# Sign of the float64 weights carried through the fp32 conversion by a parametric ReLU, with a new order of issue

## The chip, the cores and the metric

The kernel runs on one core of one Trainium2 chip. The core has TensorE (PE, with its weight loads as PEld), VectorE (DVE), ScalarE (ACT), GpSimd (POOL) and SyncE (SP), which issues the transfers. The metric is the time of one execution in microseconds on the device. The kernel before took 516.62 us, the median of 3 runs (513.7 to 518.07).

## The reference

Three blocks follow one another. An attention over 16 heads (2 batches of 8) of 768 positions and 64 dimensions masks by hash buckets; its output is laid out as two sequences of 768 x 512. A gated convolution and a mix of neighbours with a squared ReLU follow.

```python
q_bits = (einsum('bhsd,dk->bhsk', q, proj) > 0); k_bits = ...
mask = q_bucket[..., :, None] == k_bucket[..., None, :]
scores = where(mask, scale * q @ k.T, -1e9); scores -= max(scores, -1)
attn = exp(scores) / (sum(exp(scores), -1) + 1e-09);  a = attn @ v
gate = sigmoid(sum_k conv_w[k] * shifted(x, k));  y = (gate * (x @ w_val)) @ w_out
xk = mu_k * y + (1 - mu_k) * y_prev;  xr = mu_r * y + (1 - mu_r) * y_prev
v = max(xk @ w_k, 0) ** 2 @ w_v;  out = sigmoid(xr @ w_r) * v
```

The weights `w_val`, `conv_w`, `w_out`, `w_k`, `w_v` and `w_r` come as float64, and no engine computes in that type. The kernel reads each as pairs of 32-bit words, the low word (`raw[:, :, 0]`) and the high word (`raw[:, :, 1]`), and makes fp32 of them.

## The kernel before, in words

**Attention, about the first 270 us.** The heads run one after another. For each head and each of 6 tiles of 128 keys, `smax` (L685, L687) makes scores without the low parts on PE, whose maximum over all keys DVE takes out of PSUM; the 6 maxima become a shift in `mxr` (L692) that PE turns into a row (`shift`, L699, L703). Later `scores` (L713, L714) makes the exact scores of half a tile of queries, ACT takes the exponential into one of 6 buffers of a ring (L715), POOL adds up the denominators (L717, L719) and `values` (L725) multiplies by v on PE. `sums`, `spread` and `norm` (L745, L757 to L761, L775, L778) divide. Beside this, pairs of later heads are loaded, transposed (L550, L552), split into a high and a low part (`prep_hi` L556 on ACT, `prep_lo` L559 on DVE), hashed to bits (`prep_bits`: PE L564, DVE L567, ACT L569) and copied into place by transfers (`fill`, `penalties`).

**The conversion of the weights** runs in the same time: 28 tiles of 128 x 512 (`weight(i, part)`) and one of 20 x 128 for `conv_w` (`vectors`). Part 0 loads a tile into one of two `raw` buffers. Part 1, `cvt_high` (L387), is an ACT copy of the high word, read as fp32, times 2^-112, which moves the exponent by the difference of the two biases and leaves it three places too far right. Part 2, `cvt_low` (L390), is an ACT copy that scales the low word's leading bits down to an integer. Part 3, `cvt_join`, is on DVE in three steps: shift left by 3 and clear the sign bit (L394), add the low word's bits (L396, shown as CUSTOM_DVE_ANT_0), and take the sign bit from the high word and OR it in (L397).

**After it,** `split_weight` (L416, L417) splits each fp32 weight into two fp32r parts: ACT copies the high part, then DVE (tiles 0 to 7, 18, 19) or POOL (the others) subtracts. The front of the first half sequence (taps of the convolution L447, `front_val`, gate L450 to L452, `mid_out`, mixes L461 to L468) is woven into heads 13 to 15 and what follows them. From about 318 us on, four half sequences run as long chains of matmuls (`acc3`, L427, three per product of split operands).

**The order.** Every engine works through its own queue in order. `_order` gives each event a slot from constants (`K_...`) plus corrections by name in two tables (`MOVED`, and `SWING` for what repeats by head), sorts by slot, and the events are issued in that order.

Of the kernel before, what the change touches and what calls it, by code (L numbers as in the profile page):

```python
# [51 lines left out]
K_END = (3.3, 10.5, 7.4)  # L52
K_OPEN = -0.2
K_SPLIT = (5.2, 1.8)
K_SPLIT2 = (1.6, 1.75)
K_CLOSE = 8.6

K_XS = (6.3, 0)
K_TAP = (9, 0.6)
K_VAL = (2.7, 1)  # L60
K_SIG = (13.7, 0.1)
K_GATE = (14, 0.6)
K_OUT = (17.6, 0.7)
K_MIX = (8.5, 9, 0.5, 1, 13, 1.2, 0.7)
NC, NTAP, NSPLIT, NRAW, NSPLIT2 = 4, 5, 8, 12, 28
K_SPLITR = (10.2, 5.9)
# [267 lines left out]
def fused_kernel(ctx: ExitStack, tc: tile.TileContext, q, k, v, proj, w_val, conv_w, w_out,  # L334
                 mu_k, mu_r, w_k, w_v, w_r, cols, sel, out):
    nc = tc.nc
# [49 lines left out]
    def cvt_high(raw, dst):  # L386
        nc.scalar.activation(out=dst, in_=f32(raw[:, :, 1]), func=AF.Copy, scale=2.0 ** -112)  # L387
# [623 lines left out]
```

## Time and profile before

| | |
|---|---|
| median of 3 runs | 516.62 us (513.7 to 518.07) |
| the profiled execution's own time | 515.39 us |
| its span, first to last instruction | 513.6 us |
| PE, DVE, ACT, POOL busy in the span | 94%, 71%, 61%, 39% |
| TensorE clock granted, mean of the span | 0.995 of full speed |

Busy shares are means over stages with different limits; the stretches matter more. PE's matmuls overlap one another and their ends are modelled, so a busy PE can still be slowed. A wait is put down to the engine that released it last.

### The profile page before, as it was taken

Reading aid. Unit: us, or ns where it says so; the run is one execution under the profiler, and the core shown is the slowest. Engines: PE = TensorE matmul, PEld = TensorE weight load, DVE = VectorE, ACT = ScalarE, POOL = GpSimd, SP = SyncE. Lnnn points to the kernel's source line nnn. Section 1 sums busy time; section 2 is a strip of 40 time slices with the busy share of each in tenths; the row PEclk is TensorE's granted clock in tenths of the full one; section 3 lists DMA queues with packets and bytes.
Section 4 is the critical chain, followed back from the end, with each engine's and each line's share of the span. In section 5 each row is a group of like instructions: output and inputs, shape, how many; then the busy total and the mean of one; then the engine's idle time right before and its main releaser. Section 6 shows DMA issues by size and latency. Waiting matters only on the chain.

```text
span 513.6 us, 7300 instructions
## 1 busy us (share of the span) xinstructions
PE 482.3 (94%) x2545; PEld 360.6 (70%) x2545; DVE 363.7 (71%) x551; ACT 312.8 (61%) x632; POOL 198.7 (39%) x205
## 2 busy tenths in 40 slices
PE   8799989899999989999896998999999999999997
PEld 5655565564656556455575986899889998899885
DVE  4858889798999969989999992269522992138113
ACT  5868678686778687778756586275522852236221
POOL 6476656673857757667772136400000000000000
PEclk9999999999999999999999998999999999999999
DMA  7498968879789783780000000001000010001001
GB/s 171 112 213 228 231 166 187 186 202 209 198 194 217 192 208 121 201 205 2 0 2 1 2 1 2 0 1 61 1 0 2 1 63 0 1 0 63 0 1 61
DMA packets 43522, 47.57 MB, mean 93 GB/s; under 512 B 29250, under 2 KB 33886, under 8 KB 43486
## 3 DMA queue, kind: packets, MB, share of 16 engines
q1 hardware_dynamic: 43486, 47.12, 36.8%
q8 instruction: 20, 0.33, 0.3%
q14 instruction: 16, 0.13, 0.1%
HBM read 24.35 MB, written 3.15 MB: 54 GB/s over the span
## 4 chain that ended last, share of the span: by engine, by line
PE 48%; DVE 9%; ACT 3%; issue 2%; DMA 1%; POOL 1%; SPq 0%; DVEq 0%; ACTq 0%; POOLq 0%
PE bank L427 24%; PE smb L427 16%; PE bank L725 3%; DVE gp L447 3%; PE bank L713 2%; PE smb L685 1%; PE bank L714 1%; ACT ring L715 1%; DMA raw<-in_moe_w_v_dram 1%; DVE xT L778 1%; DVE mx L687 1%; DVE w L417 1%; POOL w L417 1%; DVE tm L462 1%; DVE big L439 1%
## 5 line engine op out<-in xcount | busy, mean ns | idle before, releaser
L719 POOL TENSOR_TENSOR acc<-acc,ring 128x384 f32<-128x384 f32 x128 | 131.1, 1041 | 38.1 <-ACT ring L715 35.3
L715 ACT ACTIVATE ring<-bank 128x384 f32<-128x384 f32 x192 | 89.9, 494 | 33.4 <-PE bank L714 32.4
L687 DVE TENSOR_REDUCE mx<-smb 128x1 f32<-128x768 f32 x96 | 88.6, 951 | 17.6 <-PE smb L685 16.8
L713 PE MATMUL bank<-big,big 128*128 128x384 f32 x192 | 75.0, 391 | 6.9 <-ACT ring L715 6.3
L725 PE MATMUL bank<-ring,vn 128*64 128x385 f32 x384 | 77.8, 504 | 0.9 <-ACT ring L715 0.9
L427 PE MATMUL bank<-big,w 128*128 128x384 f32 x224 | 75.5, 337 | 0.7 <-POOL w L417 0.7
L935 DVE TENSOR_TENSOR gp<-gp,bank 128x384 f32<-128x384 f32 x32 | 17.5, 550 | 75.7 <-ACT gp L934 75.7
L713 PEld LDWEIGHTS bank<-big,big 128*128 128x128 f32 x192 | 36.0, 188 | 42.8 <-ACT ring L715 22.7
L714 PE MATMUL bank<-big,big 97*128 97x384 f32 x192 | 65.0, 339 | 0.0
L427 PE MATMUL smb<-wv,kk 128*128 128x512 f32 x176 | 60.5, 391 | 0.0
L685 PE MATMUL smb<-big,big 88*128 88x384 f32 x192 | 51.0, 354 | 6.2 <-DVE mx L687 4.6
L934 ACT ACTIVATE gp<-bank 128x384 f32<-128x384 f32 x32 | 15.7, 491 | 60.7 <-PE bank L427 60.6
L717 POOL TENSOR_TENSOR acc<-ring 128x384 f32<-128x384 f32 x32 | 30.3, 950 | 47.3 <-ACT ring L715 47.2
L725 PEld LDWEIGHTS bank<-ring,vn 128*64 128x64 f32 x384 | 22.4, 135 | 31.2 <-issue 25.7
L685 PEld LDWEIGHTS smb<-big,big 88*128 88x128 f32 x192 | 32.8, 189 | 15.6 <-DVE mx L687 8.9
L427 PEld LDWEIGHTS bank<-big,w 128*128 128x128 f32 x224 | 42.0, 188 | 1.4 <-POOL w L417 1.4
L447 DVE SCALAR_TENSOR_TENSOR gp<-xT,vec,gp 128x384 f32<-128x384 f32 x64 | 41.0, 672 | 0.3
L427 PEld LDWEIGHTS smb<-wv,kk 128*128 128x128 f32 x176 | 33.2, 188 | 6.8 <-DVE kk L938 0.2
L714 PEld LDWEIGHTS bank<-big,big 97*128 97x128 f32 x192 | 36.5, 190 | 0.0
L427 PE MATMUL smb<-w,kk 128*128 128x512 f32 x88 | 34.5, 392 | 0.0
L427 PE MATMUL bank<-big,raw 128*128 128x384 f32 x128 | 33.1, 338 | 0.5 <-DVE big L468 0.5
L938 DVE TENSOR_TENSOR kk<-gp,kk 128x384 fp32r<-128x384 f32 x32 | 18.3, 576 | 20.7 <-ACT kk L937 20.5
(141 smaller groups left out, 896.6 us busy)
## 6 DMA issues: line engine op xcount, KB each, us to landing
big<-hlq SPq DMA_DIRECT2D x14, 384.0 KB
big<-hlk SPq DMA_DIRECT2D x14, 384.0 KB
raw<-in_moe_w_k_dram SPq DMA_DIRECT2D x8, 512.0 KB
raw<-in_moe_w_v_dram SPq DMA_DIRECT2D x8, 512.0 KB
vn<-in_v_dram SPq DMA_DIRECT2D x8, 384.0 KB
qn<-in_q_dram SPq DMA_DIRECT2D x14, 192.0 KB
kn<-in_k_dram SPq DMA_DIRECT2D x7, 384.0 KB
big<-bits SPq DMA_DIRECT2D x28, 96.0 KB
```

Of the source, the lines that this page charges most:

```text
L427: nc.tensor.matmul(out=ps, lhsT=w[a], rhs=xx[c], start=first and j == 0 and m == 0, stop=last and j == n - 1 and m == 2)
L447: nc.vector.scalar_tensor_tensor(out=gp, in0=src, scalar=w, in1=gp, op0=ALU.mult, op1=ALU.add)
L685: nc.tensor.matmul(out=sm[:, hf, 0:HF], lhsT=qd[0:KA, 0, 128 * t:128 * t + 128], rhs=kd[0:KA, 0, HF * hf:HF * hf + HF], start=True, stop=True)
L687: nc.vector.tensor_reduce(out=mxs[n][:, t:t + 1], in_=sm[:, :, 0:HF], op=ALU.max, axis=AX.XY)
L713: nc.tensor.matmul(out=st, lhsT=kd[:, 1, kt], rhs=qd[:, 1, cs], start=True, stop=False)
L714: nc.tensor.matmul(out=st, lhsT=kd[0:KS + 1, 0, kt], rhs=qd[0:KS + 1, 0, cs], start=False, stop=True)
L715: nc.scalar.activation(out=p[:, 0:HF], in_=st, func=AF.Exp, scale=scale)
L717: nc.gpsimd.tensor_add(acc, probs[n, 0, hf][:, 0:HF], p[:, 0:HF])
L719: nc.gpsimd.tensor_add(acc, acc, p[:, 0:HF])
L725: nc.tensor.matmul(out=pvp[n][64 * hf:64 * hf + 64], lhsT=nat["v", n // 2][:, n % 2, t, :], rhs=probs[n, t, hf], start=t == 0, stop=t == N ...
L935: nc.vector.tensor_mul(rl, rl, ps)
L938: (nc.vector if f in V_LO else nc.gpsimd).tensor_sub(kk[:, 1], rl, f32(kk[:, 0]))
```

## The change

`cvt_high` becomes a parametric ReLU with the same factor 2^-112 and a slope alpha of -(2^32) for negative inputs. A negative weight comes out positive and 2^32 times as large, so bit 28 of its pattern is set; the shift left by 3 moves that bit to the place of the sign and drops what stood above. `cvt_join` then needs neither the AND nor the third step: two DVE instructions per tile where there were three. All numbers that give the order are new, by mostly small amounts; the tables change in nearly every row. Lines of the changed file lie 23 further down from the tables on (L394 and L396 are its L420 and L421).

```diff
-K_SPLIT2 = (1.6, 1.75)
-K_CLOSE = 8.6
+K_SPLIT2 = (0.9, 2.05)
+K_CLOSE = 10
...
-K_TAP = (9, 0.6)
+K_TAP = (8.3, 0.6)
...
-    ('prep_bits', 2): -2.5, ('smax', 3, 3): -1, ('prep_hi', 'q', 2): 6, ('prep_t', 2, 'q', 0): -9,
+    ('prep_bits', 2): -2.5, ('smax', 3, 3): -1, ('prep_hi', 'q', 2): 6, ('prep_t', 2, 'q', 0): -11.4,
...
     def cvt_high(raw, dst):
-        nc.scalar.activation(out=dst, in_=f32(raw[:, :, 1]), func=AF.Copy, scale=2.0 ** -112)
+        nc.scalar.activation(out=dst, in_=f32(raw[:, :, 1]), func=AF.Prelu, scale=2.0 ** -112, alpha=-(2.0 ** 32))
...
     def cvt_join(raw, dst):
         t = dst.bitcast(I32)
-        nc.vector.tensor_scalar(out=t, in0=t, scalar1=3, scalar2=0x7FFFFFFF,
-                                op0=ALU.logical_shift_left, op1=ALU.bitwise_and)
+        nc.vector.tensor_single_scalar(out=t, in_=t, scalar=3, op=ALU.logical_shift_left)
         nc.vector.tensor_tensor(out=t, in0=t, in1=raw[:, :, 0], op=ALU.add)
-        nc.vector.scalar_tensor_tensor(out=t, in0=raw[:, :, 1], scalar=-(1 << 31), in1=t,
-                                       op0=ALU.bitwise_and, op1=ALU.bitwise_or)
```

First place, DVE's queue in the steady attention, at the first `spread` of a pair of heads; `w` is a weight tile, `rec` and `rhl` are the reciprocals of `spread`, `xT` the normed output. Before:

```order
L394 TENSOR_SCALAR w<-w 128x512
L396 ISA w<-raw,w 128x1024
L397 SCALAR_TENSOR_TENSOR w<-raw,w 128x512
L757 RECIPROCAL rec<-dn 128x12
L760 CAST rhl<-rec 128x12
L761 TENSOR_TENSOR rhl<-rec,rhl 128x12
L559 TENSOR_TENSOR hlq<-t_687,hlq 128x768
L687 TENSOR_REDUCE mx<-smb_116 128x1
L778 SCALAR_TENSOR_TENSOR xT<-pvs,vm,bank_113 64x384 x2
```

The same place in the changed kernel:

```order
L420 TENSOR_SCALAR w<-w 128x512
L421 ISA w<-raw,w 128x1024
L780 RECIPROCAL rec<-dn 128x12
L783 CAST rhl<-rec 128x12
L784 TENSOR_TENSOR rhl<-rec,rhl 128x12
L710 TENSOR_REDUCE mx<-smb_116 128x1
L582 TENSOR_TENSOR hlq<-t_678,hlq 128x768
L801 SCALAR_TENSOR_TENSOR xT<-pvs,vm,bank_113 64x384 x2
```

The third step is gone and a maximum went ahead of a `prep_lo`; the neighbours are otherwise the same. This holds for all 28 tiles.

Second place, DVE's queue at the end of attention, around the last weight tile: `wout` are splits, `big` splits of the input, `gp` taps. Before:

```order
L439 TENSOR_TENSOR big_2292<-xT,big_2292 128x384 x2
L417 TENSOR_TENSOR w<-w,wout_0_2111 128x512
L417 TENSOR_TENSOR w<-w,wout_0_2112 128x512
L439 TENSOR_TENSOR big_2292<-xT,big_2292 128x384
L394 TENSOR_SCALAR w<-w 128x512
L396 ISA w<-raw,w 128x1024
L397 SCALAR_TENSOR_TENSOR w<-raw,w 128x512
L447 SCALAR_TENSOR_TENSOR gp<-xT,vec,gp 128x384
L757 RECIPROCAL rec<-dn 128x12
L760 CAST rhl<-rec 128x12
L761 TENSOR_TENSOR rhl<-rec,rhl 128x12
L447 SCALAR_TENSOR_TENSOR gp<-xT,vec,gp 128x384 x7
```

And in the changed kernel:

```order
L462 TENSOR_TENSOR big_2260<-xT,big_2260 128x384
L780 RECIPROCAL rec<-dn 128x12
L783 CAST rhl<-rec 128x12
L784 TENSOR_TENSOR rhl<-rec,rhl 128x12
L440 TENSOR_TENSOR w<-w,wout_0_2085 128x512
L462 TENSOR_TENSOR big_2260<-xT,big_2260 128x384
L470 SCALAR_TENSOR_TENSOR gp<-xT,vec,gp 128x384
L440 TENSOR_TENSOR w<-w,wout_0_2086 128x512
L420 TENSOR_SCALAR w<-w 128x512
L421 ISA w<-raw,w 128x1024
L470 SCALAR_TENSOR_TENSOR gp<-xT,vec,gp 128x384 x9
```

The reciprocals of heads 12 and 13 now stand ahead of the last two splits and the first tap ahead of the last tile; the taps follow in one run.

Third place, ACT's queue just before the long chains of matmuls, where the splits of `w_k` (`wk`) and `w_r` (`wr`) are made between the mixes (`tm`, `big`) and the ReLUs (`gp`). Before:

```order
L416 CAST wk_1_2652<-w 128x512
L461 ACTIVATE tm<-xT,omm 128x384
L934 ACTIVATE gp<-bank_112 128x384
L465 CAST big_2696<-tm 128x384
L461 ACTIVATE tm<-xT,omm 128x384
L465 CAST big_2696<-tm 128x384
L416 CAST wk_1_2653<-w 128x512
L416 CAST wr_0_2654<-w 128x512
L416 CAST wr_0_2655<-w 128x512
```

And in the changed kernel:

```order
L439 CAST wk_1_2643<-w 128x512
L484 ACTIVATE tm<-xT,omm 128x384
L957 ACTIVATE gp<-bank_112 128x384
L488 CAST big_2667<-tm 128x384
L439 CAST wk_1_2644<-w 128x512
L439 CAST wr_0_2645<-w 128x512
L484 ACTIVATE tm<-xT,omm 128x384
L957 ACTIVATE gp<-bank_114 128x384
L488 CAST big_2667<-tm 128x384
L439 CAST wr_0_2646<-w 128x512
```

The fourth cast of `wk` and the first of `wr` went one step of the mix ahead; POOL subtracts behind each of these casts.

## Rows read from the trace of the kernel before

**Rows 1.** The page: span, busy time by engine, chain that ended last.
```profile
span 513.6 us, 7300 instructions
PE 482.3 (94%) x2545; PEld 360.6 (70%) x2545; DVE 363.7 (71%) x551; ACT 312.8 (61%) x632; POOL 198.7 (39%) x205
PE 48%; DVE 9%; ACT 3%; issue 2%; DMA 1%; POOL 1%; SPq 0%; DVEq 0%; ACTq 0%; POOLq 0%
```

**Rows 2.** Windows: length, busy us of PE, PEld, DVE, ACT, POOL (instructions), clock, DMA.
```profile
0.00:40.00 40.00, 33.54 (x190) 22.12 (x190) 25.59 (x35) 27.00 (x50) 23.51 (x37) 1.00 0.72 169
40.00:140.00 100.00, 92.16 (x511) 54.91 (x513) 86.92 (x114) 75.35 (x154) 64.33 (x64) 1.00 0.82 199
140.00:240.00 100.00, 95.55 (x538) 56.76 (x534) 89.28 (x120) 77.51 (x156) 66.58 (x69) 1.00 0.71 175
240.00:300.00 60.00, 53.18 (x279) 40.04 (x277) 58.88 (x95) 38.79 (x85) 25.65 (x23) 1.00 0.01 1
300.00:318.00 18.00, 16.00 (x73) 13.50 (x73) 9.77 (x17) 14.45 (x30) 10.13 (x8) 0.91 0.00 0
318.00:513.60 195.60, 191.84 (x964) 173.30 (x962) 93.27 (x174) 79.71 (x162) 8.54 (x7) 1.00 0.05 17
```

**Rows 3.** Waits from 20 to 240 us: waiter, releaser, us in total, times, longest.
```profile
PE smb L685 <- DVE mx L687: 3.5, 6, 1.5
PE smb L699 <- DVE mxr L692: 1.6, 2, 1.1
PE bank L745 <- DVE bits L567: 0.5, 2, 0.3
ACT bits L569 <- DVE bits L567: 9.9, 7, 2.7
PE bank L713 <- ACT ring L715: 5.7, 15, 0.9
PE smb L685 <- DMA big<-bits: 1.5, 1, 1.5
```

**Rows 4.** Groups by line and form: count, busy us, mean ns, idle before.
```profile
L713 PE MATMUL bank<-big,big 128*128 128x384 f32 x192 | 75.0, 391 | 6.9 <-ACT ring L715 6.3
L714 PE MATMUL bank<-big,big 97*128 97x384 f32 x192 | 65.0, 339 | 0.0
L397 DVE SCALAR_TENSOR_TENSOR w<-raw,w 128x512 int32<-128x512 int32 x28 | 25.8, 922 | 1.0
L394 DVE TENSOR_SCALAR w<-w 128x512 int32<-128x512 int32 x28 | 16.3, 582 | 2.8 <-ACT w L387 2.7
L387 ACT ACTIVATE w<-raw 128x512 f32<-128x512 f32 x28 | 21.9, 783 | 4.9 <-DMA raw<-in_moe_w_val_dram 2.9 <-DMA raw<-in_moe_w_v_dram 0.7 <-DMA raw<-in_moe_w_k_dram 0.6
L848 ACT ACT_TABLE_LOAD x1 | 1.3, 1283 | 0.0
```

**Rows 5.** Windows of L397 alone on DVE: length, busy us (instructions), clock, DMA.
```profile
40.00:140.00 100.00, 12.66 (x13) 1.00 0.82 199
140.00:240.00 100.00, 11.21 (x13) 1.00 0.71 175
240.00:300.00 60.00, 0.69 (x1) 1.00 0.01 1
```

**Rows 6.** L397's durations (ns min/median/max), and timelines of DVE and POOL (start, us).
```profile
L397 DVE SCALAR_TENSOR_TENSOR w<-raw,w x28: 691/693/1520, 32.1 to 255.5; 128x512 int32<-128x512 int32 x28
172.06 1.52 DVE L397 SCALAR_TENSOR_TENSOR w<-raw,w 128x512 int32<-128x512 int32 x1
172.03 1.01 POOL L719 TENSOR_TENSOR acc<-acc,ring 128x384 f32<-128x384 f32 x1 [1.17 <-ACT ring L715]
...
238.21 0.69 DVE L397 SCALAR_TENSOR_TENSOR w<-raw,w 128x512 int32<-128x512 int32 x1
```

**Rows 7.** Waits from 303 to 319 us, and the window of the slower clock.
```profile
PE bank L427 <- POOL w L417: 2.0, 4, 0.9
314.00:318.00 4.00, 3.85 (x10) 3.04 (x11) 1.38 (x2) 2.33 (x6) 2.26 (x3) 0.57 0.01 2
```

More of the change, by code (lines that the diff above doesn't have):

```diff
@@ new lines @@
+    ('shift', 0, 0): -1.8, ('scores', 1, 5, 0): -1.7, ('scores', 1, 3, 0): -0.6, ('shift', 0, 1): 1.3,
+    ('norm', 0): 0.3, ('scores', 1, 0, 1): -0.3, ('values', 0, 5): 1, ('scores', 0, 5, 1): -0.2,
+    ('weight', 2, 2): 0.5, ('weight', 1, 2): 1, ('weight', 0, 3): 0.5, ('weight', 2, 1): 0.5, ('smax', 1, 4): -0.3,
+    ('scores', 1, 1, 0): -0.8, ('scores', 0, 3, 0): 1, ('values', 0, 2): 0.5, ('scores', 0, 1, 1): 0.7,
+    ('weight', 0, 2): 0.5, ('scores', 0, 2, 0): 0.5, ('weight', 1, 0): 0.1,
@@ new lines @@
+    ('prep_t', 2, 'k', 0): -2.1, ('first_hi', 0, 1): 7, ('values', 15, 3): 7.2, ('smax', 2, 0): -1.2,
+    ('values', 13, 2): 0.2, ('smax', 2, 1): 1.1, ('weight', 0, 1): -17.9, ('values', 15, 0): 5.7,
+    ('spread', 14, 1): 1.3, ('prep_lo', 'k', 2): 3.3, ('fill', 3, 0): 15, ('first_bits', 0): -12.3,
+    ('prep_lo', 'q', 1): 4, ('shift', 1): -1.5, ('warm', 4): -4, ('values', 14, 4): -1.9, ('values', 13, 5): 3.5,
+    ('first_hi', 0, 0): -13.8, ('weight', 3, 0): 5, ('weight', 0, 2): -7.6, ('norm', 11): 0.8, ('weight', 1, 3): 4.4,
@@ new lines @@
+    ('load_qk', 5): -0.3, ('shift', 2): -0.3, ('load_v', 7): 3, ('values', 15, 2): 6.7, ('values', 15, 4): 5.7,
+    ('values', 15, 5): 5.7, ('warm', 8): 0.8, ('weight', 9, 2): -2.4, ('weight', 9, 0): -0.7, ('weight', 9, 1): -1.2,
+    ('weight', 9, 3): -0.7, ('prep_hi', 'q', 5): -0.7, ('shift', 4): -0.3, ('weight', 1, 1): -0.9,
+    ('prep_t', 1, 'k', 0): 0.5, ('weight', 26, 0): -1, ('weight', 17, 2): -1.5, ('smax', 2, 5): 3,
+    ('penalties', 2): 0.3, ('prep_lo', 'q', 6): -0.5, ('weight', 14, 0): -0.1, ('weight', 21, 3): -0.3,
@@ new lines @@
+    ('weight', 8, 0): -1.8, ('weight', 8, 2): -4, ('weight', 8, 3): -0.7, ('prep_hi', 'q', 7): 0.5,
+    ('penalties', 6): 2.6, ('smax', 8, 0): -1.8, ('prep_t', 5, 'k', 0): 0.5, ('smax', 14, 3): 2.7,
+    ('fill', 15, 1): -0.3, ('weight', 24, 3): -1.5, ('weight', 24, 0): -0.7, ('weight', 24, 1): -4.7,
+    ('weight', 24, 2): -2.2, ('load_v', 5): -6.9, ('shift', 0, 0): 1, ('scores', 13, 4, 1): -1.7,
+    ('scores', 14, 0, 0): -0.8, ('scores', 1, 4, 1): -1.3, ('weight', 6, 0): -1, ('scores', 0, 5, 0): -0.6,
@@ new lines @@
+    ('norm', 1): 0.3, ('scores', 11, 5, 1): -1, ('mid_hi', 1, 2): 0.8, ('weight', 18, 0): -1.5,
+    ('scores', 5, 4, 1): 1.3, ('sums', 13): 0.9, ('mid_lo', 1, 1): 1.5, ('front_gate', 2): 1.2,
+    ('weight', 27, 2): 0.3, ('weight', 13, 3): -0.3, ('scores', 4, 3, 0): 1.3, ('fill', 8, 1): 3,
+    ('scores', 8, 4, 1): 1.2, ('vectors', 2): -2, ('scores', 4, 5, 0): 0.5, ('shift', 6): 1,
+    ('prep_t', 3, 'q', 1): 0.3, ('weight', 6, 3): 0.3, ('weight', 18, 2): -0.7, ('mid_hi', 1, 3): 0.7,
+    ('shift', 11): -0.7, ('weight', 21, 2): -0.7, ('scores', 4, 4, 0): 0.8, ('prep_lo', 'k', 6): 0.4,
```

297 lines of the change are left out of this document (148 added, 149 removed).

## The prediction

> **What bounds the kernel now.** I began with the page's busy times and its chain [rows 1]: PE is busy 94% of the span and holds 48% of it on the chain that ended last, DVE 9%. That alone would say that work taken from DVE is worth nothing. So I cut the span into stretches [rows 2]. From 318 us on PE is busy 191.84 of 195.6 us and DVE 93; nothing in this change touches that part. Before it three stretches differ. From 40 to 240 us PE is busy 187.71 of 200 us, DVE 176.20 and ACT 152.86: no engine is full, three in-order queues hand work to each other, and PE is idle for 12.3 us. From 240 to 300 us DVE is busy 58.88 of 60 us and PE only 53.18: here DVE sets the pace. From 300 to 318 us neither does; ACT is busy 14.45 of 18 us and PE waits for POOL [rows 7].
>
> The waits say who holds PE up in the second stretch and its run-up [rows 3]. From 20 to 240 us PE waits for DVE's maxima, shifts and bits for 3.5 + 1.6 + 0.5 = 5.6 us, for ACT's exponentials 5.7 us. Behind ACT stands DVE once more: in each of 7 pairs of heads ACT's scaling of the bits waits for DVE, 9.9 us in all, and ACT's exponentials queue behind it. A wait also costs more than its idle time: the first matmul of a score takes 391 ns and the second, which never waits, 339 ns [rows 4], 192 times 52 ns, or 10.0 us. What a better fed PE could win before 240 us is thus bounded by 12.3 + 10.0 = 22.3 us.
>
> **The change part by part.** *The third step.* 28 instructions of 922 ns, 25.8 us of DVE, go [rows 4]; 23.87 us of that lie from 40 to 240 us and 0.69 us after 240 [rows 5]. DVE's load from 40 to 240 us falls from 176.2 to 152.3 us, that is from 88% to 76%, ACT's level. What is it worth at the end? Between 0 (PE keeps its pace, since it is held by ACT and by its own stream) and 22.3 us (all that PE loses there). I take a value near the named waits. PE's 5.6 us of waits for DVE come in pieces of at most 1.5 us, about as long as one third step that stands ahead in the queue; with a conversion ahead of about two waits in three I let 3.5 us go. ACT's wait for the bits is 9.9 / 7 = 1.4 us each time; one third step less ahead of it saves about 0.7 us, 5 us of ACT's time, and since ACT is busy three quarters of the time I let a third of it reach PE: 1.5 us. Together -5.0 us.
>
> Part of the 922 ns is no work. L397 takes 691 ns at the least and 1520 at the most, and the long one at 172.06 us ran while POOL added from 172.03 us on [rows 6]. So 28 times 0.69, or 19.3 us, is work, and 6.5 us is time held up beside POOL, which the next DVE instruction may meet instead. This is why I stay at 5.0 us and don't go higher. The Trainium skill says of this, in "SBUF — State Buffer", section "SBUF: two separate sides", that a DVE instruction with two SBUF inputs and a GpSimd instruction that reads SBUF lock each other out for a whole instruction; the trace agrees with the 691 and 1520 ns above. By that rule the lock outlives the change, as the add (L396) still takes it, and the saving would be 19.3 / 25.8 of what was counted, 3.7 us instead of 5.0.
>
> *The first step with one operation instead of two.* L394 takes 582 ns on average [rows 4]. The trace holds no shift alone; the nearest row is L394 itself, so I put 0 and bound it by 28 times its whole 0.58 us to either side: -16.3 us of DVE's time if it cost nothing, +16.3 if it doubled. Neither extreme has a reason, since input and output are the same; over the path the ratio taken above (5.0 of 25.8) makes this -3 to +3 us.
>
> *ReLU for copy on ACT.* 28 instructions of 783 ns [rows 4], same shape, factor and operands. I put 0. The bounds are again from the nearest row: -21.9 to +21.9 us of ACT (free or doubled); ACT is a quarter idle, so at most some 7 us of that would reach the end. A table switch would be dearer; it is the fourth rival.
>
> *The stretch led by DVE.* The last tile's third step (0.69 us) goes from it, and that of the tile ahead of it, 0.69 us at 238.21 us [rows 6], hands DVE over to this stretch that much earlier; the only third step behind 240 us is the last tile's [rows 5]. DVE is full here, so both count whole: -1.4 us. The reciprocals that now go first only reorder DVE's work; their gain is that PE's norm of heads 12 and 13 is ready sooner, which I put at 0. What comes late next is the run of taps, which is as long as before.
>
> *The new order before 318 us.* The casts of the fourth `wk` and the first `wr` go one step of the mix ahead on ACT, and so do POOL's subtractions behind them. PE waited 2.0 us in four pieces for these [rows 7]; I take half of it, -1.0 us. The bounds are -2.0 us and, if the ReLUs that now queue behind the casts came late, +1.6 us (two casts, each at most the 0.78 us of L387, the nearest row [rows 4]). Right behind the last of these waits the granted clock was 0.57 on average from 314 to 318 us, partly the lower level of 1.2 GHz, after PE had waited again and again. I don't count on its going.
>
> *All other moves* shift events by at most a few halves of a score tile. Loads and fills stay in the same places between the heads, SP's queue moves with them. I put 0, and -2 to +2 us for what a start with other neighbours may do in the first 40 us, where PE is idle 6.46 us [rows 2].
>
> Sum: -5.0 - 1.4 - 1.0 = -7.4 us against the profiled execution, 515.4 us: 508.0 us. The median of the runs shown is 1.2 us above that execution, which gives 509.2; I say 509 us.
>
> **The rivals.** *1. The time was hidden.* DVE's idle time grows and PE keeps its pace, as ACT's exponentials and PE's stream set it. For it speaks that PE is already busy 95.55 of 100 us from 140 to 240 us and waits for ACT as long as for DVE [rows 2, 3]; against it that ACT itself waits 9.9 us for DVE. Only the 1.4 us at the end remain: 515.4 - 1.4 + 1.2 = 515 us.
>
> *2. DVE set the pace all along.* Of the 23.87 us two thirds come back, 16 us, below the bound of 22.3. For it speak 88% of load on a queue with waits at both ends; against it the named waits, which are a third of that. 515.4 - 16 + 1.2 gives 501 us.
>
> *3. Slower: the transfers come late.* The 16 DMA engines are busy 82% from 40 to 140 us [rows 2], and once there a maximum waited 1.5 us for the bits of the next pair to land [rows 3]. If the heads run on faster while fills and penalties are issued as late as before, PE comes 7.4 / 7 = 1.1 us earlier to each of 7 pairs, and a pair that waits then costs 1.5 + 1.1 = 2.6 us. From three such pairs on (7.8 us) the gain is eaten; with five it is 13.0 - 7.4 = 5.6 us slower, 522 us. Against it: one such wait in seven pairs.
>
> *4. The ReLU isn't in the exponential's table.* Each of 28 conversions would then load a table twice, at 1283 ns [rows 4]: 72 us of ACT. ACT is idle for 47 us from 40 to 240 us [rows 2], so 25 to 72 us would show: 541 to 589 us, in the middle 565. The queue of the changed kernel has still two table loads, at its start and ahead of the first sigmoid, as before, which nearly excludes it. The Trainium skill, "ScalarE: Activation LUTs", section "Table sets: the hidden batching unit", says that functions are loaded in named sets and a change of set costs a load; two loads in both queues agree with one common set.
>
> **How the numbers follow.** The forecast has 0.55, and its own range is 504 to 512 us. Rival 1 has 0.25, rival 2 has 0.11, rival 3 has 0.08, rival 4 has 0.01. From 501 to 517 us takes in the forecast, rival 1 and half of rival 2, and the bounds of the small terms; rival 3 and the far half of rival 2 stay out. About 1%, or 5 us, is what a measurement of this kernel can tell from no change. Faster by more than that: four fifths of the forecast and rival 2 and a little of rival 1, 0.58. Slower: most of rival 3 and rival 4, 0.07. Within 1%: 0.35.
>
> **What would show it.** In the profile after, DVE should have 28 large instructions fewer and some 25 us less busy time, near 338 us; the shift should keep its 582 ns and the ReLU its 783 ns. PE's waits for DVE's maxima from 20 to 240 us should fall from 5.6 to about 2 us, ACT's wait for the bits from 9.9 to about 5, and the last score should come 5 us earlier. Waits of PE for ACT that grow by as much as those for DVE fall would prove rival 1; waits for the bits' transfers in most pairs rival 3; a last score 15 us earlier rival 2. A longer ReLU or shift would make a term of the sum wrong.

## The result, and the profile after

The changed kernel takes 510.46 us (median of 4 runs, 509.83 to 511.14), the kernel before beside it 515.64 us (4 runs): ratio 0.9897, 95% interval 0.9849 to 0.9945, or -5.2 us (509.0 were forecast). Its profiled execution took 510.76 us with a span of 509.0 us; before it was 515.39 and 513.6. Run again later on another chip, the same kernel took 508.69 us, ratio 0.9907 (0.9873 to 0.9942), or -3.0 to -6.5 us; the two medians there differ by 6.6 us (515.31 before). A few runs below took over 1.5% longer than the fastest of the same kernel: the ratios leave them out, the medians don't.

The page after, in the same lines as [rows 1]:

```profile
span 509.0 us, 7262 instructions
PE 485.2 (95%) x2545; PEld 360.1 (71%) x2545; DVE 335.5 (66%) x522; ACT 314.4 (62%) x632; POOL 192.7 (38%) x205
PE 55%; DVE 6%; ACT 5%; DMA 1%; issue 1%; POOL 1%; SPq 0%; ACTq 0%; POOLq 0%; DVEq 0%
```

DVE has 29 instructions and 28.2 us less and holds 6% of the chain, not 9. PE's busy time went up by 2.9 us although it has the same 2545 matmuls; the windows, cut as in [rows 2], tell why:

```profile
0.00:40.00 40.00, 34.19 (x188) 22.11 (x189) 23.19 (x32) 28.37 (x52) 22.28 (x37) 0.96 0.79 186
40.00:140.00 100.00, 94.41 (x516) 55.13 (x516) 74.22 (x102) 75.20 (x152) 61.69 (x66) 0.98 0.82 194
140.00:240.00 100.00, 97.27 (x544) 58.11 (x540) 80.50 (x111) 80.07 (x161) 66.39 (x69) 1.00 0.70 174
240.00:300.00 60.00, 56.14 (x290) 41.86 (x290) 56.00 (x93) 39.88 (x86) 26.11 (x24) 1.00 0.01 1
300.00:318.00 18.00, 15.97 (x76) 13.18 (x76) 9.58 (x17) 13.57 (x28) 11.58 (x10) 1.00 0.01 2
318.00:509.00 191.00, 187.25 (x944) 169.68 (x942) 92.01 (x171) 77.28 (x157) 4.68 (x4) 1.00 0.05 17
```

The clock was 1.00 in both of the first windows of [rows 2] and 0.91 from 300 to 318 us. Now it is 0.96 and 0.98 at the start and 1.00 from 300 to 318: the stretches at the lower level of 1.2 GHz, half of the full 2.4 GHz, have moved into the attention. There a matmul counts as busy for longer (the second one of a score 0.52 us at 124.78 us, 0.34 us at 120.41), so part of PE's higher share is no gain. From 40 to 240 us DVE is busy 154.72 of 200 us, 77%; before it was 88%.

The waits from 20 to 240 us, in answer to [rows 3], and the groups, in answer to [rows 4]:

```profile
PE bank L736 <- ACT ring L738: 5.5, 13, 1.2
ACT bits L592 <- DVE bits L590: 3.5, 6, 1.3
PE smb L708 <- DMA raw<-in_moe_w_k_dram: 1.4, 1, 1.4
PE smb L722 <- DVE mxr L715: 0.7, 2, 0.4
PE smb L708 <- DMA big<-bits: 0.5, 1, 0.5
PE smb L708 <- DVE mx L710: 0.2, 1, 0.2
```

```profile
L736 PE MATMUL bank<-big,big 128*128 128x384 f32 x192 | 76.1, 396 | 6.6 <-ACT ring L738 6.3
L413 ACT ACTIVATE w<-raw 128x512 f32<-128x512 f32 x28 | 22.2, 791 | 2.9 <-DMA raw<-in_moe_w_k_dram 1.5 <-DMA raw<-in_moe_w_v_dram 1.3
L420 DVE TENSOR_SCALAR w<-w 128x512 int32<-128x512 int32 x28 | 14.2, 509 | 2.7 <-ACT w L413 2.7
L421 DVE CUSTOM_DVE_ANT_0 w<-raw,w 128x1024 uint16<-128x1024 uint16 x28 | 26.0, 928 | 6.6 <-ACT raw L416 3.6 <-DMA big<-bits 0.2
```

The wait of the shifts for the maxima fell from 1.6 to 0.7 us, that of the maxima's matmuls for DVE from 3.5 to 0.2 us, and ACT's wait for the bits from 9.9 to 3.5 us. These are the waits the forecast named. But the first matmul of a score is no faster (396 against 391 ns), and PE's wait for ACT's exponentials stays (5.5 against 5.7 us). PE's wait for transfers, 1.5 us in the kernel before, is 1.9 us now and stands at another place. Before, it came at 96 us (first line), now where the maxima of the fifth pair begin:

```profile
96.17 0.44 PE L685 MATMUL smb<-big,big 88*128 88x384 f32 x1 [1.52 <-DMA big<-bits]
123.42 0.41 PE L708 MATMUL smb<-big,big 88*128 88x384 f32 x1 [1.42 <-DMA raw<-in_moe_w_k_dram]
124.28 0.44 PE L708 MATMUL smb<-big,big 88*128 88x384 f32 x1 [0.45 <-DMA big<-bits]
```

These matmuls read `big` alone, where the penalties write the hash bits (big<-bits). The raw weight tile that the second line names is read as one that landed at the same time, and both waits as waits for the penalties.

```profile
29.00:32.00 3.00, 2.95 (x11) 1.42 (x13) 1.81 (x3) 1.26 (x4) 1.20 (x2) 0.52 0.97 196
...
120.00:124.00 4.00, 2.41 (x15) 1.01 (x13) 1.24 (x3) 2.18 (x5) 2.55 (x3) 1.00 1.01 222
124.00:128.00 4.00, 3.72 (x11) 1.95 (x11) 2.63 (x3) 1.14 (x3) 1.00 (x1) 0.58 1.02 214
```

From 120 to 124 us PE works 2.41 of 4 us while the 16 DMA engines are full (1.01); right behind it the granted clock is 0.58, partly the lower level. DVE works 1.24 of these 4 us and ACT 2.18: the core waits for bytes. Behind the wait at 96 us in the kernel before the clock stayed at 1.00. What SP had issued ahead of these bytes stands in its timeline:

```profile
107.79 0.70 SPq L558 DMA_DIRECT2D kn<-in_k_dram  x1
109.62 0.34 SPq L406 DMA_DIRECT2D raw<-in_moe_w_k_dram  x1
110.01 0.64 SPq L687 DMA_DIRECT2D big<-hlq  x1
...
115.60 0.66 SPq L698 DMA_DIRECT2D big<-bits  x1
...
118.25 0.59 SPq L700 DMA_DIRECT2D big<-bits  x1
```

The last of the four penalty transfers is issued at 118.25 us and waited for until 124 us, though the four carry only 0.1 MB each: keys, a raw weight tile and four fills of 0.2 to 0.4 MB are ahead of them. So the questions were: what is the conversion worth by itself, what the new order; is DVE still worth relieving; and does this stall cost the rest of the forecast?

### The profile page after: what moved, and what is told of

It is laid out like the page before. It is cut to its first block, busy times and chain, and to the rows that moved or that the text cites. A ratio compares the mean times of both kernels' runs of the same rounds, so it can differ in the third digit from the quotient of the medians.

```text
span 509.0 us, 7262 instructions
## 1 busy us (share of the span) xinstructions
PE 485.2 (95%) x2545; PEld 360.1 (71%) x2545; DVE 335.5 (66%) x522; ACT 314.4 (62%) x632; POOL 192.7 (38%) x205
## 4 chain that ended last, share of the span: by engine, by line
PE 55%; DVE 6%; ACT 5%; DMA 1%; issue 1%; POOL 1%; SPq 0%; ACTq 0%; POOLq 0%; DVEq 0%
PE bank L450 23%; PE smb L450 18%; PE bank L748 5%; PE bank L736 3%; PE bank L737 2%; PE smb L708 2%; ACT ring L738 2%; DVE gp L470 1%; DMA big<-hlq 1%; DVE tm L485 1%; POOL w L440 1%; DVE xT L801 1%; DVE mx L710 1%; PE bank L768 1%; ACT tm L484 0%
## 5 line engine op out<-in xcount | busy, mean ns | idle before, releaser
L742 POOL TENSOR_TENSOR acc<-acc,ring 128x384 f32<-128x384 f32 x128 | 125.8, 997 | 49.0 <-ACT ring L738 46.3
L736 PE MATMUL bank<-big,big 128*128 128x384 f32 x192 | 76.1, 396 | 6.6 <-ACT ring L738 6.3
L450 PE MATMUL bank<-big,wk 128*128 128x384 f32 x128 | 32.9, 337 | 0.0
```

Source lines behind the costliest of these rows:

```text
L450: nc.tensor.matmul(out=ps, lhsT=w[a], rhs=xx[c], start=first and j == 0 and m == 0, stop=last and j == n - 1 and m == 2)
L736: nc.tensor.matmul(out=st, lhsT=kd[:, 1, kt], rhs=qd[:, 1, cs], start=True, stop=False)
L742: nc.gpsimd.tensor_add(acc, acc, p[:, 0:HF])
```

## The experiments

Each was timed in 5 rounds against the kernel before on the same chip; times are medians, ratios have 95% intervals. The first four share a chip, the next four another and the three behind them a third; the last has its own.

**The conversion alone, in the old order.**

```diff
-        nc.scalar.activation(out=dst, in_=f32(raw[:, :, 1]), func=AF.Copy, scale=2.0 ** -112)
+        nc.scalar.activation(out=dst, in_=f32(raw[:, :, 1]), func=AF.Prelu, scale=2.0 ** -112, alpha=-(2.0 ** 32))
...
-        nc.vector.tensor_scalar(out=t, in0=t, scalar1=3, scalar2=0x7FFFFFFF,
-                                op0=ALU.logical_shift_left, op1=ALU.bitwise_and)
+        nc.vector.tensor_single_scalar(out=t, in_=t, scalar=3, op=ALU.logical_shift_left)
...
-        nc.vector.scalar_tensor_tensor(out=t, in0=raw[:, :, 1], scalar=-(1 << 31), in1=t,
-                                       op0=ALU.bitwise_and, op1=ALU.bitwise_or)
```

> The kernel before with the new conversion alone (parametric ReLU, two steps on DVE), in the old order. Hidden (the 25.8 us of DVE are worth little before the last score, and the 5.2 us of the change come mostly from the new order): ratio 0.995 to 0.998, that is -1 to -2.5 us, with the last score within 1.5 us of its old place, 267.7 us. Conversion (the freed time is what pays, the order only follows): 0.989 to 0.992, -4 to -5.5 us, and the last score at 265 us or earlier. Only together (the old order can't use the freed time): 0.998 or above.

Measured: 510.13 us, 0.9893 (0.9861 to 0.9925): as much as the whole change (0.9897). The four runs that the ratio counts have a median of 508.99 us; against 515.16 beside it the saving is thus between 5.0 and 6.2 us. In its profile (span 506.2 us) the scores' second matmul runs last at 261.7 us, 6.1 us earlier than before. The windows from 40 us on, the waits, and that matmul's first and last start:

```profile
40.00:140.00 100.00, 95.42 (x535) 57.30 (x535) 75.86 (x105) 78.52 (x158) 62.41 (x66) 1.00 0.82 204
140.00:240.00 100.00, 96.57 (x536) 57.36 (x532) 80.46 (x111) 78.37 (x162) 65.67 (x70) 1.00 0.68 170
```

```profile
ACT bits L566 <- DVE bits L564: 5.7, 6, 1.4
PE smb L682 <- DVE mx L684: 0.9, 2, 0.5
```

```profile
L711 PE MATMUL bank<-big,big x192: 332/340/346, 22.4 to 261.7; 97*128 97x384 f32 x192
```

At full clock PE does 24 more matmuls from 40 to 140 us than before (535 against 511 recorded). ACT's wait for the bits, 9.9 us before, is 5.7; the maxima's for DVE went from 3.5 to 0.9. The expectation "conversion" holds. PE's wait of the shifts for the maxima is unchanged here, 1.6 us.

**The new order alone, with the old conversion** (the diff's last part taken back).

> The changed kernel's order with the old conversion (copy, three steps on DVE). Hidden: most of the gain stays, 0.991 to 0.995. Conversion: none of it stays, 0.998 to 1.002. Only together: slower than before, 1.003 or more, because the order puts DVE's work where only a lighter DVE can do it in time; PE's waits for DVE from 20 to 240 us then rise above the 5.6 us of before.

Measured: 511.59 us, 0.9931 (0.9907 to 0.9956). The order is worth 3.6 us with the heavy DVE too. That fits "hidden", as the run before it fits "conversion", so neither theory stands: -5.0 alone and -3.6 alone give -5.2 together, and the two parts overlap. The waits show one place:

```profile
ACT bits L595 <- DVE bits L593: 5.5, 6, 1.6
...
PE smb L711 <- DVE mx L713: 0.9, 2, 0.6
```

With the order alone ACT waits 5.5 us for the bits and the maxima 0.9 us for DVE, almost as with the conversion alone. Both parts shorten the same waits. In PE's time the order alone shows less of this: head 14 begins 1.55 us earlier than before (234.69 us against 236.24), with 2.0 us of waits for big<-bits ahead of it, and of the 3.8 us by which the span (509.8 us) is shorter more than half is won behind that.

**The third step put back for the last two tiles.**

```diff
+        if third:
+            nc.vector.scalar_tensor_tensor(out=t, in0=raw[:, :, 1], scalar=-(1 << 31), in1=t,
+                                           op0=ALU.bitwise_and, op1=ALU.bitwise_or)
...
-                cvt_join(raws.pop(i), w32[w_tiles[i]])
+                cvt_join(raws.pop(i), w32[w_tiles[i]], i >= 26)
```

> The changed kernel with the third step put back for the last two of the 28 tiles alone (weights stay right, as there the sign is set twice). My term of 1.4 us for the stretch that DVE leads: 1.2 to 1.6 us slower than the changed kernel, ratio to before near 0.9925, and the shift is there at the first matmul of the long chains. If DVE doesn't set the pace of that stretch: no difference, 0.9895 to 0.990.

Measured: 509.38 us, 0.9889 (0.9855 to 0.9923), no slower than the changed kernel. From head 14's first score (231.42 us) to the end of the span (506.7) it takes 275.3 us, the changed kernel 274.9: of 1.4 us of DVE 0.4 us are seen, and the time can't tell them.

**The old order from head 13 on**, the new one ahead of it (slot 156 is head 13's start; the diff shows the rule, the kernel has the list that it gives).

```diff
-    return [e[2:] for e in sorted(events, key=lambda e: e[:2])]
+    return [e[2:] for e in sorted((n if n[0] < 156 else o for n, o in zip(new, old)), key=lambda e: e[:2])]
```

> The changed kernel with its own order up to the start of head 13 and the order of before from there on (new conversion). If the new order behind the attention pays (casts and splits earlier, reciprocals first): 2 to 3 us slower than the changed kernel, ratio 0.994 to 0.996, last score unchanged at 265.3 us and the first matmul of the long chains at 314 to 315 us in place of 312.1. If the gain behind the last score is the conversion's: no difference, 0.989 to 0.991.

Measured: 510.93 us, 0.9916 (0.9890 to 0.9941): between the expectations, and too near the changed kernel to tell apart by the time. The profiles tell more. From head 14's first score to the first wr matmul, timelines of before, of the conversion alone, of this kernel and of the changed one:

```profile
236.24 0.45 PE L713 MATMUL bank<-big,big 128*128 128x384 f32 x1
310.82 0.40 PE L427 MATMUL bank<-wr,big 128*128 128x512 f32 x1
```

```profile
230.90 0.45 PE L710 MATMUL bank<-big,big 128*128 128x384 f32 x1
304.13 0.40 PE L424 MATMUL bank<-wr,big 128*128 128x512 f32 x1
```

```profile
233.62 0.45 PE L814 MATMUL bank<-big,big 128*128 128x384 f32 x1
306.85 0.40 PE L528 MATMUL bank<-wr,big 128*128 128x512 f32 x1
```

```profile
234.09 0.34 PE L736 MATMUL bank<-big,big 128*128 128x384 f32 x1
305.79 0.40 PE L450 MATMUL bank<-wr,big 128*128 128x512 f32 x1
```

That is 74.6 us before, 73.2 with the new conversion and the old order (in both kernels that have it), and 71.7 with both. So the conversion gives 1.4 us here in the old order, the new order 1.5 us more. But behind this mark the new order takes longer: 203.2 us to the end of the span, 202.1 with the conversion alone. Counted from head 14's first score to the end of the span it is 277.4 us before, 275.3 with the conversion alone, 276.0 in this kernel, whose clock fell between 308 and 316 us, and 274.9 in the changed one (274.8 in its second profile): the conversion gives 2.1 us with the fall of the clock that went with it, the new order 0.4 to 1.1.

**The changed kernel again** (no edit; the comparison for the next three).

> The changed kernel once more, beside the three that follow, for a comparison on one chip. The first experiments' profiles say: conversion alone wins 5 to 6 us before head 14 and 1.4 us behind it; the new order wins 1.5 us more behind it but loses as much in the first 40 us and at 121 to 128 us, where the clock falls to its lower level. 0.988 to 0.992, with the clock at the lower level at 29 us again (0.5) in the profiled run.

Measured: 508.69 us, 0.9907; the clock fell at 30 to 33 us again. This profile (span 505.6 us) has no fall at 125 us, only 0.4 us of waiting for the bits there, and its last score is 3.3 us earlier than in the first profile of the same kernel (262.2 against 265.5). So the stall comes and goes between runs. The mean clock of the ten runs of the changed kernel says how often: five with 0.995 or more, this profile (0.996) among them, took 507.37 to 509.83 us, five with 0.993 or less, the first profile (0.993) among them, 510.16 to 511.74 us.

**The old order up to head 13, the new one behind it** (the sorting of the fourth experiment with new and old exchanged, new conversion).

> The new conversion in the old order up to the start of head 13 and in the new order from there on. If the new order's gain lies behind head 13 and its loss ahead of it: this is the fastest, 1.0 to 2.0 us below the conversion alone and the changed kernel, ratio 0.985 to 0.988; the clock stays at 1.0 at 29 and at 125 us; from head 14's first score to the first wr matmul 71.7 us (73.2 with the old order). If the two parts of the change merely relieve the same waits and the place doesn't matter: 0.989 to 0.991, as the others.

Measured: 511.16 us, 0.9926 (0.9897 to 0.9954). My expectation fell: not the fastest. Its profile has PE waiting 2.1 us for big<-bits at the same place as the changed kernel's, and the lower clock at 126 to 130 us. The clock stayed at 1.0 at 29 us and the stretch from head 14 to the first wr matmul takes 71.5 us, as expected. The place of the loss isn't the new order's: the old order meets it as well, once DVE is light. Up to head 13 this kernel is the conversion alone, whose profile had no such stall: here too it comes and goes.

**The old order in the first 18 slots** (the same sorting with 18 for 156).

> The changed kernel with the order of before in the first 18 slots (one and a half heads, up to some 45 us) and its own from there on. If the new start causes the fall of the clock at 29 us: none there, and head 2 starts 0.4 to 1 us earlier than 55.1 us; the time is 1.0 to 1.5 us below the changed kernel's. If the fall at 29 us is chance, it comes again and the time is the same as the changed kernel's within 0.5 us.

Measured: 511.97 us, 0.9935 (0.9908 to 0.9961): not faster; the median is 3.3 us above the changed kernel's. The clock stays at 1.0 at 29 us, so the new start does bring that fall, and head 2 starts at 54.4 us, 0.7 us earlier than in the changed kernel's first profile. But the gain is lost at the fifth pair, where this PE arrives earlier still:

```profile
120.00:124.00 4.00, 1.89 (x13) 0.87 (x13) 0.49 (x2) 1.46 (x3) 1.98 (x3) 0.90 1.05 228
124.00:128.00 4.00, 4.00 (x11) 2.06 (x11) 2.69 (x3) 1.57 (x3) 1.00 (x1) 0.50 1.01 210
128.00:132.00 4.00, 4.00 (x13) 2.61 (x13) 0.96 (x1) 1.13 (x4) 1.97 (x3) 0.50 0.56 128
```

PE works 1.89 of 4 us, then runs at half clock for 8 us and more; only one of its twelve runs has a mean clock of 0.995 or more. What is won ahead of a late transfer is lost at it, and the clock falls besides.

**The second DVE step left out too.** The low word's part of the weights is missing here.

```diff
-        nc.vector.tensor_tensor(out=t, in0=t, in1=raw[:, :, 0], op=ALU.add)
```

> The changed kernel without the second DVE step too: the low word's part of the weights (their last bits) is left out, 28 adds of 928 ns or 26.0 us of DVE's time. If DVE's load still set the pace, as it did for the third step (about 4 to 5 us for 25.8 us of DVE): another -3 to -5 us, 0.980 to 0.984. If what was left is ACT's and PE's own stream (rival 1, from here on): within 1 us of the changed kernel.

Measured: 506.26 us, 0.9847 (0.9815 to 0.9879), 2.4 us below the changed kernel beside it, between the expectations; the intervals overlap. The two profiles, first the changed kernel's, then this one's, with spans of 505.6 and 505.3 us:

```profile
140.00:240.00 100.00, 97.36 (x541) 58.08 (x541) 81.63 (x110) 80.08 (x163) 68.54 (x70) 1.00 0.68 171
```

```profile
140.00:240.00 100.00, 97.30 (x541) 57.92 (x541) 72.14 (x100) 80.48 (x163) 67.37 (x70) 1.00 0.68 171
```

Another 9.5 us of DVE less in this window, and PE does the same 541 matmuls in the same time. Where nothing is late, DVE is off the path in the new order; the old order was not tried with so light a DVE.

**The third step done twice, in the kernel before.**

```diff
+        nc.vector.scalar_tensor_tensor(out=t, in0=raw[:, :, 1], scalar=-(1 << 31), in1=t,
+                                       op0=ALU.bitwise_and, op1=ALU.bitwise_or)
```

> The kernel before with its third DVE step done twice (an or with the same bits: the weights stay the same), 28 more instructions, some 20 to 26 us of DVE. If DVE's load sets the pace at its level of before (88% from 40 to 240 us): slower by 4 us or more, 1.008 to 1.02, and DVE over 95% busy in that stretch. If the saving had been hidden: within 1 us, 0.998 to 1.002.

Measured: 537.0 us, 1.0439 (1.0411 to 1.0466), +22 us: the direction expected, but more than twice the 2% that I gave as the upper end. DVE's busy time grew by 28.9 us (392.6 against 363.7), so three quarters as much is seen at the end:

```profile
140.00:240.00 100.00, 87.43 (x477) 50.10 (x475) 93.99 (x121) 68.59 (x140) 64.13 (x61) 1.00 0.66 169
```

```profile
PE smb L687 <- DVE mx L689: 13.0, 16, 1.7
PE smb L701 <- DVE mxr L694: 3.9, 5, 1.5
```

DVE is at 94%, not over the 95% that I expected, and PE's wait for maxima is 13.0 us where it was 3.5. Part of the 22 us comes by way of the clock: from 40 to 140 us its mean is 0.95 (1.00 before), by my estimate up to 5% of those 100 us, or 5 us. The kernel before thus stood at a bend: +28.9 us of DVE cost 22 us, -27.3 us (the conversion alone) gave 5.0 to 6.2, and a further 26.8 (308.9 against 335.7, in the new order) gave 2.4 by the medians, with intervals that overlap.

**q and k of the sixth pair loaded later**, behind the fifth pair's penalties.

```diff
-    ('load_qk', 5): -0.3
+    ('load_qk', 5): 7
```

> The changed kernel with one move: the loads of q and k of the sixth pair (qn, kn, 0.77 MB) are issued 7.3 slots later, behind the penalties of the fifth pair, not ahead of them. Theory: a lighter DVE brings PE earlier to head 6's maxima, whose penalties (big<-bits) land late among these loads; PE then stands still at 121 to 125 us in some runs and the clock falls. Then here: no wait of PE for big<-bits over 0.2 us from 112 to 136 us, no lower clock there, head 7 at 131 us or earlier in the profile, median 1 to 2 us below the changed kernel's, ratio 0.986 to 0.989, and the spread of its runs within 2.5 us. Rival (the stall has another cause, or the transfers only move): 0.9895 to 0.9915 and the wait there or at the next pair.

Measured: 510.99 us, 0.9932 (0.9908 to 0.9957), not below the changed kernel. Half of the theory holds: the wait for big<-bits and the fall at 125 us are gone, and head 7 starts at 129.1 us. But now what stands behind these loads is late (waits from 115 to 140 us):

```profile
ACT hlq L579 <- DMA big<-hlq: 3.0, 1, 3.0
PE bank L736 <- ACT ring L738: 3.0, 1, 3.0
```

ACT can't overwrite hlq until the fills have read it, its exponentials queue behind that, and PE stands for 3.0 us until 133 us; then the clock falls. The rival named in the expectation holds: the transfers only moved, and with them the wait.

**The same with the old start.** The sorting with 18, on top of that move.

> The same move, with the order of before in the first 18 slots as in the experiment with the old start. Theory: the old start keeps the clock up at 29 us (it did), and without the late transfers its 1 us reaches the end: 0.984 to 0.987, below the changed kernel's by 2 us or more, median near 507 us. If the old start costs something else: not below the one with the move alone.

Measured: 512.52 us, 0.9963 (0.9937 to 0.9990). My expectation fell again; PE waits 3.4 us at the same place, and the clock falls there and at 51 us. The fall at 51 us follows a wait of 1.8 us for ACT's exponentials; the same wait, 1.8 us at 49 us, stands in the profile of the old start without that move, and there the clock stayed at 1.00 up to 56 us.

**One raw weight tile loaded behind the penalties**, its conversion up to 4.5 slots later.

```diff
-    ('weight', 12, 3): 0.1
-    ('weight', 12, 1): -3.6, ('weight', 12, 0): -3.6, ('weight', 12, 2): -1.4
+    ('weight', 12, 3): 0.6
+    ('weight', 12, 1): 0.9, ('weight', 12, 0): 3.25, ('weight', 12, 2): 0.9
```

> The changed kernel with one transfer less ahead of the fifth pair's penalties: the load of the 13th weight tile (0.5 MB) is issued just behind them, and its conversion 0.5 to 4.5 slots later; q and k of the sixth pair stay where the changed kernel has them. Theory of the late transfers: no wait of PE over 0.2 us for big<-bits from 112 to 136 us, clock at 1.0 there, head 7 starts by 131 us and ACT doesn't wait over 0.5 us for big<-hlq, as it did with q and k late; the time is 1 to 2 us below the changed kernel's, 0.985 to 0.989. Rival (the transfers there are one bunch, and whatever goes late is waited for): 0.990 to 0.993, with a wait of 1 us or more for a raw tile or for big<-hlq between 120 and 140 us.

Measured: 507.01 us, 0.9854 (0.9829 to 0.9878), five runs between 506.17 and 508.59 us: the lowest ratio of all kernels that do the whole work, and well below before. Against the changed kernel (0.9897 and 0.9907) the intervals still touch, 0.9878 above here and 0.9873 below there. The same windows as after's:

```profile
120.00:124.00 4.00, 3.63 (x24) 2.00 (x22) 2.95 (x4) 2.56 (x5) 2.50 (x3) 1.00 0.87 253
124.00:128.00 4.00, 3.35 (x19) 1.81 (x16) 2.68 (x4) 2.87 (x6) 1.63 (x2) 1.00 1.06 233
```

No wait for transfers is left among PE's from 112 to 136 us, ACT doesn't wait for hlq, the clock stays at 1.00. Head 7 starts at 131.4 us, 2.0 us earlier than in the changed kernel's first profile (131.0 in its second, which had no stall). Its five runs all have a mean clock of 0.995 or more, where five of ten of the changed kernel's have; this, more than the one profile, speaks for the half megabyte in SP's queue as the stall, but the runs are few. The move isn't free: PE now waits 0.6 us for big<-bits at the next pair's maxima, at 155.6 us, and the last score comes at 263.5 us, 1.3 us later than in the changed kernel's second profile. The Trainium skill, "DMA: Bandwidth & Descriptors", section "Queues, rings and completion order", says that each DMA engine takes up what one issuing engine gave it in the order of the ring. This run agrees: with 0.5 MB less ahead of the penalties they were in time. It is no proof: the tile's conversion moved along with its load, which was not tried apart, and with the tile in its place the second profile of the changed kernel waited only 0.4 us.

## Why the prediction was right, and where its sum was off

*The third step, -5.0 us.* Right, by its own mechanism. The conversion alone, for which the sum gives -5.0 - 1.4 = -6.4 us, measures between -5.0 and -6.2 us; in its profile head 14 begins 5.3 us earlier (230.90 against 236.24), and the two named waits shrank, ACT's for the bits from 9.9 to 5.7 us ("about 5") and PE's for the maxima from 3.5 to 0.9. Rival 1's sign, a longer wait for ACT's exponentials, didn't come (5.3 us there, 5.5 in the changed kernel, 5.7 before). Ratio of path to work: 5.0 to 6.2 of 27.3 us. What I hadn't seen is how sharp the bend is: with DVE loaded by one more such step, leaving that step out again is worth 22 us, part of it clock. The upper bound of 22.3 us was itself too high. It counted 10.0 us as waiting because the first matmul of a score takes longer than the second, but the first is as slow where the waits are shorter (392 ns with the conversion alone, 396 in the changed kernel). From the changed kernel's 82% of DVE (140 to 240 us) down to 72% PE gains nothing more in that window, which is rival 1's picture, beginning just behind the change.

*The lock beside POOL.* By the rule that the prediction cites from the Trainium skill, "SBUF — State Buffer", section "SBUF: two separate sides", the saving would have been 3.7 us, since the add would meet the time held up. In the changed kernel the add does take longer: 928 ns on average, 835 before (L396). With the conversion alone, in the old order, it takes 801 ns. DVE's busy time fell by more than the third step's 25.8 us in both (28.2 and 27.3). In the changed kernel the shift took back 2.1 of the 2.6 us that the add gained (509 ns on average, 582 before); with the conversion alone it did not (593 ns), and there the add itself is shorter. So the long instances move from one instruction to another with the order, and the held-up time didn't eat the saving; 5.0 stands nearer than 3.7.

*The shift with one operation and the ReLU for the copy, 0 each.* Right: the ReLU 791 ns against 783, the shift's median 419 ns against 416 with two operations. Rival 4 is out: two table loads, as before, and the ReLU as long as the copy.

*The stretch led by DVE, -1.4 us, and the new order ahead of 318 us, -1.0.* Together -2.4 us forecast; measured from head 14 to the end 277.4 to 274.9, -2.5 us. But they are not two sums of one account: up to the first wr matmul the conversion gives its 1.4 in the old order; in the new order two third steps put back cost 0.4. And the mechanism of the -1.0 is not there. PE's waits for POOL from 303 to 319 us, which I let fall by half, are 2.0 us as before:

```profile
PE bank L450 <- POOL w L440: 1.7, 3, 0.9
PE smb L450 <- POOL w L440: 0.3, 1, 0.3
```

What went is the lower clock behind them (1.00 from 314 to 318 us, 0.57 before), on which I hadn't counted. It is gone with the conversion alone too, but not with the old order from head 13 on, so the wait alone doesn't set it.

*What was missing: a fourth term, with a plus.* The part of the sum that failed is the price of rival 3, which it left out. I counted a late pair only from three pairs on and gave it 0.08 as a case of its own. It is no case apart from the forecast but a term in it. The kernel before already had one late pair (1.5 us at 96 us, no fall of the clock behind it). In the changed kernel that wait is gone, and in some of the runs another stands at the fifth pair: 1.9 us of waiting (2.6 forecast), and a fall of the clock behind it that I hadn't priced. Without that stall the profiles show the forecast or more: spans of 506.2 us for the conversion alone and 505.6 for the change, -7.4 and -8.0 against 513.6, which holds a fall of its own [rows 7]; but each of the two is the fastest run of its kernel. With one tile's load moved the median is 7.2 us lower than before (507.01 against 514.23). That the runs of the changed kernel are mixed is shown by its two profiles (a last score at 265.5 and at 262.2 us; the forecast was 5 us earlier than the 267.8 of before), and the mean clocks of the ten fit; where in the runs without a profile the clock fell is not known.

*Other moves, 0.* Not right, and here the forecast had luck. The order alone, conversion left out, measures -3.6 us where the sum gives the new order -1.0; on top of the conversion it gives next to nothing (0.9897 and 0.9907 against 0.9893). The total came out near because the two overlap, which the sum didn't foresee. At the start the order costs: it lets the clock fall between 29 and 33 us in seven of the eight profiles that have it, the old start in none of six. From the old start I expected 1 to 1.5 us and got none; the profile shows the time won being lost at the fifth pair. With that pair's transfers in time and the old start kept, it wasn't tried.

## What to carry to other kernels

Relieving an engine is worth what its queue's neighbours still wait for, and the slope has a bend: test it from both sides, by doing the removed step twice and by leaving out one more, before putting a rate on it. A new order and a lighter engine that shorten the same waits don't add. When a stage gets faster, look at every transfer issued just ahead of the next thing PE needs: a big load that isn't needed yet, standing ahead of a small one that is, can take the gain back, and moving another one of the bunch may only move the stall, as q and k did here.

## What the hardware showed that I hadn't expected

A single wait of PE of 1.4 to 3.4 us was followed by half clock in five profiles: at 125 us (changed kernel), 126 (old order up to head 13), 123 (old start), 133 (q and k late) and 136 us (q and k late with the old start); with the old order from head 13 on, waits of 1.0 and 0.5 us were followed by it at 126 us. It was not followed by it each time: 1.5 us at 96 us in the kernel before and 1.8 us at 49 us with the old start left the clock at 1.00. Nor is it the transfers that bring it: with the third step done twice PE worked 2.28 of the 4 us from 120 to 124 us, waiting for maxima, and the clock was 0.57 in the next 4.

Such a fall can cost more than the waits say. From head 6 to head 7 the changed kernel takes 20.4 us with it (113.1 to 133.4 us) and 17.5 without (113.5 to 131.0), 2.9 us more for 1.5 us more of waiting for transfers. Time and mean clock of the runs of one kernel go together: on one chip the kernel before took 511.98 and 513.10 us with a mean clock of 1.000, and 516.24 to 518.57 us in the six runs with 0.989; on another 512.06 to 514.15 us in four runs with 1.000, 514.62 and 519.47 in the two with 0.989. A difference of a few us between single profiles must be read with that column beside it.
